# A DRAM copy of the filters in the order of its reading, read back in fewer, taller transfers, the first third at an earlier place

## The chip, the cores and the metric

The kernel runs on one core of a Trainium2 chip. The metric is the device time of one execution in microseconds (us), as the median over several runs. A profile is one profiled execution; its trace has every instruction of every engine and every DMA packet. The engines are named as in the profile: PE (TensorE), PEld (its weight loads), DVE (VectorE), ACT (ScalarE), POOL (GpSimd) and SP (SyncE, which issues DMAs here and computes nothing).

## The reference, cut to what matters

```python
x = (8, 3008, 256); filt_r, filt_i = (1505, 256)      # 3008 = 47 * 64
X = np.fft.rfft(x, axis=1)
y = np.fft.irfft(X * (filt_r + 1j * filt_i), n=3008, axis=1)      # mixing along the sequence
h = y.reshape(24064, 256) @ w_in                       # 256 -> 2048
out = (0.5 * h * (1 + erf(h / sqrt(2)))) @ w_out       # exact GELU, 2048 -> 256
```

Each of 8 batches is transformed along its sequence, multiplied by a filter for each frequency and channel, and transformed back. The result goes through a two-layer network with GELU.

## The kernel before

The transform of length 3008 = 47 x 64 is made of matrix products in stages. A batch of index 1 to 7 goes through these functions:

- `s1` (L375) makes the first products from x, evacuates them through `a_sb` (three buffers, L43) and stores them to a DRAM tile R, 16 transfers a batch (L397). R is read back in another order by `r1` into `b_sb`, four transfers (L403).
- `s2` (L406) makes the spectrum for two of 24 frequency rows at a time, so there are 12 calls a batch, p = 0 to 11. DVE multiplies each by the filters, straight out of PSUM (L414).
- `s3` (L417) and `s3_out` (L434) make the next products and store them through `v_sb` to a second DRAM tile R. `r2` (L442) reads them into `d_sb`, and `s4` (L450) writes y into the ring `y_sb`.

Batch 0 takes another way without DRAM tiles: `c1`, `c1t`, `c2`, `c3`, `c3t`, `c4`. Its twelve products by the filters are in `c2` (L489).

The network follows in 47 tiles of 512 rows: `mm1` (L562) makes `ps_h`, which ACT turns into `g_sb` with GELU, and `mm2` or `mm2_seven` (L575, L642) make the output, which DVE adds up in `ost` and SP stores. The stages of batch b+1 are spread between the products of the network for batch b. That order is written out by hand: each of the 48 x 16 slots of the last loop has a list of calls, which `put(slot, function, arguments)` fills, and each slot ends with a piece of `mm2` and one of `mm1`. Every engine, and SP's queue, runs its instructions in the order in which they are written; nothing is reordered.

The filters lie in one SBUF tile `F` of 128 partitions x 2 (real, imaginary) x 24 rows (`K1`) x 256 channels. Batch 0 and the others need it in different partition orders:

- `load_filters` (L88) loads 64 partitions from the inputs on POOL's queue: rows 0 to 31 direct, 32 to 63 mirrored. `dup_filters` (L110) copies them to partitions 64 to 127. Batch 0 uses F in that order.
- `save_filters` (L97) stores partitions 0 to 63 to a DRAM tile `Fd`, one transfer of 1536 KB on SP (L99).
- `load_filters_again` (L101) reads `Fd` back into F in the order that batches 1 to 7 need: even or odd rows by half of F, each group of 32 rows twice. Each transfer fills 16 partitions from every second row of `Fd`, so a call issues 8 transfers on SP (L107).

The call for rows 0 to 7 stands at slot 13 and that for rows 8 to 23 at slot 17. For batch 1 the four steps of `s1` stand at slots 0, 4, 8 and 12, the first three `r1` at slot 15, and `s2` from slot 22 on. So SP's queue holds, in this order: the save of the filters, 16 stores of R, 8 filter transfers of 128 KB, three loads of `b_sb`, 8 filter transfers of 256 KB, and then an output store, the fourth load of `b_sb`, another output store and the stores of `v_sb`.

F's rows 0 to 7 serve the products p = 0 to 3, rows 8 to 23 the products p = 4 to 11.

Of the kernel before, what the change touches and what calls it, by code (L numbers as in the profile page):

```python
# [12 lines left out]
BF16 = mybir.dt.bfloat16  # L13
# [6 lines left out]
K1 = 24  # L20
# [10 lines left out]
class _Mix:  # L31
# [62 lines left out]
            for q, a in enumerate((direct, mirror)):  # L94
                nc.gpsimd.dma_start(out=self.F[32 * q:32 * q + 32, t, k0:k0 + k, :], in_=a)

    def save_filters(self):  # L97
        self.Fd = self.dram.tile([64, 2, K1, 256], BF16, tag="Fd", name="Fd")
        self.nc.sync.dma_start(out=self.Fd, in_=self.F[0:64])  # L99

    def load_filters_again(self, k0, k):  # L101

        for par in range(2):
            for r in range(2):
                for q in range(2):
                    o = 64 * par + 32 * r + 16 * q
                    self.nc.sync.dma_start(out=self.F[o:o + 16, :, k0:k0 + k, :],  # L107
                                           in_=self.Fd[32 * q + (par ^ q):32 * q + 32:2, :, k0:k0 + k, :])

    def dup_filters(self, eng, k0, k):  # L110
        for k in range(k0, k0 + k, 2):
# [582 lines left out]
def kernel(  # L694
# [9 lines left out]
    m = _Mix(ctx, tc, x, filt_r, filt_i, moe_w_in, moe_w_out, out)  # L704
# [38 lines left out]

    nc.gpsimd.memset(m.vt[:, :, 96, :], 0.0)
    m.dup_filters(nc.gpsimd, 4, 20)
    m.save_filters()


    m.table_2_sin(0)
# [31 lines left out]
    for q in range(1, 7):  # L781
        if q < 6:
            m.c2(2 * q)
            if q + 2 < 6:
                m.c1t(q + 2, (act,))
            if q != 3:
                m.warm_up(2)
            m.c2(2 * q + 1)
        if q < 6:
            m.c3(2 * q - 2)  # L790
            if q == 3:
                m.table_3(2)
                m.table_3_copy(2, True)
            else:
                m.warm_up(1)
        else:
            m.c3(10, 1)
            m.warm_up(1)
            m.c3(11, 1)
# [20 lines left out]
    def put(slot, f, *a):  # L820
        at.setdefault(slot, []).append((f, a))
# [30 lines left out]
    put(7, m.table_4_factors, g)  # L852
    put(11, m.table_u)
    put(11, m.table_4_all, g)
    put(13, m.load_filters_again, 0, 8)
    put(17, m.load_filters_again, 8, 16)
    put(17, m.weight_sums)
    seven = range(1, NT - 1)
# [6 lines left out]
    for s in range((NT + 1) * 16):  # L865
        t, jc = s // 16, s % 16
# [37 lines left out]
```

## Time and profile before

| what | value |
|---|---|
| median of 3 runs | 766.86 us (766.77 to 769.4) |
| the profiled execution's own time | 767.05 us |
| its span, first to last instruction | 765.3 us |
| PE busy | 733.2 us (96%) |
| DVE busy | 585.7 us (77%) |
| ACT busy | 545.5 us (71%) |
| POOL busy | 101.1 us (13%) |
| SP's DMA queue (hardware), share of 16 engines | 36.6% of the span, 73.43 MB |
| POOL's DMA queue (software) | 14.2%, 16.00 MB |
| `Fd<-F`, 1 transfer of 1536 KB | 10.5 us from issue to landing |
| `F<-Fd`, 8 transfers of 128 KB | 5.3 us in the median |
| `F<-Fd`, 8 transfers of 256 KB | 13.7 us in the median |

Times inside a profile are counted from the span's start. A line of a timeline has start, length, engine, source line, operation, what it writes and reads, sizes, the number of instructions merged, and in brackets how long the engine stood idle before it and what ended that. SPq and POOLq mark the issue of a DMA; the time to landing is from issue until the last byte is there. A line of busy times by stage has the stage, its length, then the busy time and count of PE, PEld, DVE, ACT and POOL, the granted share of TensorE's clock, the mean busy share of the 16 DMA engines (over 1 where packets overlap), and GB/s. The chain of waits is followed back from the last instruction, at each step to what released it.

### The profile page before, as it was taken

How to read it: one execution, taken by the hardware profiler on the slowest of the kernel's cores; microseconds unless marked ns; L12 is line 12 of the kernel's file. 1: busy time of each engine (PE TensorE's matmuls, PEld its weight loads, DVE VectorE, ACT ScalarE, POOL GpSimd, SP SyncE). 2: the span in 40 equal slices, each digit the busy share in tenths (PEclk: the TensorE clock that was granted, in tenths of full speed). 3: DMA queues.
4: the chain of work that ended last, by engine and by line, in shares of the span. 5: the costliest groups of instructions: out<-in, count | busy, mean ns of one | idle time of the engine just before them, and what ended most of it. 6: DMA issues, size and time to landing. Idle time of an engine off the chain costs nothing.

```text
span 765.3 us, 20030 instructions
## 1 busy us (share of the span) xinstructions
PE 733.2 (96%) x8252; PEld 520.0 (68%) x8388; DVE 585.7 (77%) x1051; ACT 545.5 (71%) x963; POOL 101.1 (13%) x191
## 2 busy tenths in 40 slices
PE   7986699999999999999999999999999999999998
PEld 4834467667677667676677676766767766777776
DVE  8964597789777996789778797778977799666562
ACT  7873377766787677876778676876678767777773
POOL 7997000012000210002000120001200000000000
PEclk9998899999999999999999999999999999999999
DMA  9999935556625556337544465364662522601011
GB/s 152 220 184 168 182 90 134 142 131 114 159 62 149 120 126 134 88 115 168 114 98 125 138 142 115 90 162 112 114 159 61 148 77 84 140 28 57 29 56 56
DMA packets 91500, 90.71 MB, mean 119 GB/s; under 512 B 7632, under 2 KB 78416, under 8 KB 91088
## 3 DMA queue, kind: packets, MB, share of 16 engines
q1 hardware_dynamic: 83024, 73.43, 36.6%
q0 software_dynamic: 8384, 16.00, 14.2%
q8 instruction: 65, 1.06, 0.6%
q14 instruction: 27, 0.22, 0.1%
HBM read 57.15 MB, written 48.23 MB: 138 GB/s over the span
## 4 chain that ended last, share of the span: by engine, by line
PE 79%; DMA 8%; DVE 4%; issue 3%; POOL 2%; ACT 2%; SPq 1%; DVEq 0%; POOLq 0%; ACTq 0%
PE ps_o L657 35%; PE ps_h L570 33%; PE ps_s L456 3%; PE ps_s L428 3%; PE ps_s L411 2%; DMA F<-Fd 2%; ACT g_sb L573 2%; PE ps_s L387 2%; DVE p L414 2%; DMA x_sb<-in_x_dram 2%; DVE s_sb L627 1%; DMA b_sb<-R 1%; DMA R<-v_sb 1%; DMA d_sb<-R 1%; DMA F<-in_filt_i_dram 1%
## 5 line engine op out<-in xcount | busy, mean ns | idle before, releaser
L573 ACT ACTIVATE g_sb<-ps_h 128x512 f16<-128x512 f32 x752 | 448.2, 598 | 200.8 <-PE ps_h L570 171.0
L570 PE MATMUL ps_h<-y_sb,w_in_sb 128*128 128x512 bf16 (+3 forms) x1468 | 419.7, 366 | 1.2 <-DVE a_sb L297 1.1
L657 PEld LDWEIGHTS <-g_sb 128*128 128x128 f16 x2880 | 190.7, 98 | 85.2 <-issue 16.2
L657 PEld LDWEIGHTS <-s_sb 128*128 128x128 f16 x2160 | 147.9, 98 | 51.5 <-issue 3.1
L657 PE MATMUL ps_o<-w_sums,g_sb 128*128 128x128 f16 x1440 | 125.5, 220 | 6.8 <-DVE g_sb L633 6.0
L570 PEld LDWEIGHTS <-w_in_sb 128*128 128x128 bf16 x1600 | 125.1, 98 | 8.1 <-issue 2.4
L414 DVE TENSOR_TENSOR p<-ps_s,F 128x1024 bf16<-128x1024 f32 x84 | 102.4, 1220 | 33.9 <-PE ps_s L411 16.9
L657 PE MATMUL ps_o<-w_sums,s_sb 128*128 128x128 f16 x1440 | 125.0, 219 | 1.3
L657 PE MATMUL ps_o<-w_out_sb,g_sb 128*128 128x128 f16 x1440 | 118.4, 219 | 1.8
L627 DVE TENSOR_TENSOR s_sb<-g_sb 128x1024 f16<-128x1024 f16 x180 | 118.7, 682 | 0.0
L118 POOL COPY gate<-p 1x1 bf16<-1x1 bf16 x40 | 19.1, 477 | 438.4 <-DVE p L414 438.4
L657 PE MATMUL ps_o<-w_out_sb,s_sb 128*128 128x128 f16 x720 | 62.2, 219 | 0.5
L633 DVE TENSOR_TENSOR g_sb<-s_sb,g_sb 128x1024 f16<-128x1024 f16 x90 | 61.7, 686 | 1.1
L640 DVE TENSOR_TENSOR s_sb<-g_sb 128x1024 f16<-128x1024 f16 x90 | 61.3, 681 | 0.0
L299 DVE TENSOR_SCALAR y_sb<-ps_s 128x376 bf16<-128x376 f32 x56 | 30.5, 545 | 29.0 <-PE ps_s L456 29.0
L297 DVE CAST a_sb<-ps_s 128x512 bf16<-128x512 f32 x60 | 38.5, 685 | 16.8 <-PE ps_s L387 13.9
L456 PEld LDWEIGHTS <-d_sb 96*128 96x128 bf16 x448 | 31.4, 98 | 27.2 <-issue 2.4
L675 DVE TENSOR_TENSOR t_sb<-t_sb,ps_o 128x256 f32<-128x256 f32 x45 | 18.8, 417 | 40.3 <-PE ps_o L657 40.3
L672 DVE TENSOR_TENSOR ost<-t_sb,ps_o 128x256 f32<-128x256 f32 x45 | 18.8, 419 | 31.6 <-PE ps_o L657 31.6
L411 PE MATMUL ps_s<-b_sb,T2p 128*128 128x256 bf16 x168 | 32.6, 276 | 9.0 <-DMA b_sb<-R 8.0
L456 PE MATMUL ps_s<-T4a,d_sb 96*128 96x94 bf16 x448 | 37.4, 206 | 2.6 <-DMA d_sb<-R 1.3
L680 DVE TENSOR_TENSOR ost<-t_sb,ps_o 128x256 f32<-128x256 f32 x90 | 33.6, 414 | 7.4 <-PE ps_o L657 7.4
(149 smaller groups left out, 515.3 us busy)
## 6 DMA issues: line engine op xcount, KB each, us to landing
out_dram<-ost SPq DMA_DIRECT2D x93, 256.0 KB, 2.8
x_sb<-in_x_dram POOLq DMA_DIRECT2D x64, 188.0 KB, 4.0
R<-a_sb SPq DMA_DIRECT2D x112, 96.0 KB, 2.2
b_sb<-R SPq DMA_DIRECT2D x28, 384.0 KB, 4.4
R<-v_sb SPq DMA_DIRECT2D x84, 128.0 KB, 2.4
d_sb<-R SPq DMA_DIRECT2D x56, 192.0 KB, 4.1
F<-Fd SPq DMA_DIRECT2D x8, 256.0 KB, 13.7
Fd<-F SPq DMA_DIRECT2D x1, 1536.0 KB, 10.5
```

Of the source, the lines that this page charges most:

```text
L297: self.nc.vector.tensor_copy(out=out, in_=in_)
L299: self.nc.vector.tensor_scalar(out=out, in0=in_, scalar1=scale, scalar2=None, op0=ALU.mult)
L411: nc.tensor.matmul(ps[:, 256 * i:256 * i + 256], lhsT=self.T2p[:, k].rearrange("p a b c d -> p (a b c d)"), rhs=self.st[b, "b", k // 6][:, ...
L414: nc.vector.tensor_tensor(out=w, in0=ps.unsqueeze(1).to_broadcast([128, 2, 512]), in1=self.F[:, :, 2 * p:2 * p + 2, :].rearrange("p t a b ...
L456: nc.tensor.matmul(ps[:, 94 * i:94 * i + 94], lhsT=d[:, (grp % 2) * 4 + i, 128 * half:128 * half + 128], rhs=self.T4a[:, 4 * grp + i], sta ...
L570: nc.tensor.matmul(ps[:, o:o + n], lhsT=self.w_in_sb[:, dc, jc * 128:jc * 128 + 128], rhs=self.ring[:, dc, off:off + n], start=(dc == 0), ...
L573: nc.scalar.activation(out=self.st["g", t][:, jc, :], in_=ps, func=AF.Gelu)
L627: self.nc.vector.tensor_tensor(out=self.st["s", t][:, i:i + 2], in0=a, in1=b, op=ALU.subtract)
L633: self.nc.vector.tensor_tensor(out=a21[:, k], in0=self.st["s", t][:, k, 0], in1=a22[:, k], op=ALU.add)
L640: self.nc.vector.tensor_tensor(out=self.st["s4", t][:, k], in0=a12[:, k], in1=s2[:, k], op=ALU.subtract)
L657: nc.tensor.matmul(ps[:, (m + 1) % 2, sub, :], lhsT=a[:, i, 128 * sub:128 * sub + 128], rhs=b[:, i], start=i == 0, stop=i == 7)
L680: v(out=c(h, 1 - h), in0=tt, in1=p, op=ALU.add)
```

## The change

`Fd` gets the order in which it is read: first even or odd rows, then direct or mirrored, then 16 rows. `save_filters` takes a range of rows and makes four transfers of 32 partitions each; it is called for rows 12 to 23 and then 0 to 11, so 8 transfers of 192 KB stand for the one. For the mirrored half the rows are stored with even and odd exchanged (`o[:, ::-1]`). `load_filters_again` now fills 64 partitions with one transfer, whose source names its 32 rows twice, by a broadcast dimension in front; a call issues four transfers, of 256 KB each for rows 0 to 7 and of 512 KB for rows 8 to 23. The first call is moved from slot 13 into the loop of batch 0's products, behind the sixth of its twelve, so that in SP's queue its transfers stand between the save and the stores of R. The second call stays at slot 17. The instructions of PE, DVE, ACT and POOL and their order stay as they are.

```diff
-    def save_filters(self):
-        self.Fd = self.dram.tile([64, 2, K1, 256], BF16, tag="Fd", name="Fd")
-        self.nc.sync.dma_start(out=self.Fd, in_=self.F[0:64])
+    def save_filters(self, k0, k):
+
+        if "Fd" not in self.st:
+            self.st["Fd"] = self.dram.tile([2, 2, 16, 2, K1, 256], BF16, tag="Fd", name="Fd")
+        for t in range(2):
+            for q in range(2):
+                o = self.st["Fd"][:, q, :, t, k0:k0 + k, :].rearrange("a i k c -> i a (k c)")
+                if q:
+                    o = o[:, ::-1]
+                self.nc.sync.dma_start(out=o, in_=self.F[32 * q:32 * q + 32, t, k0:k0 + k, :])
 
     def load_filters_again(self, k0, k):
 
         for par in range(2):
-            for r in range(2):
-                for q in range(2):
-                    o = 64 * par + 32 * r + 16 * q
-                    self.nc.sync.dma_start(out=self.F[o:o + 16, :, k0:k0 + k, :],
-                                           in_=self.Fd[32 * q + (par ^ q):32 * q + 32:2, :, k0:k0 + k, :])
+            for t in range(2):
+                i = self.st["Fd"][par, :, :, t, k0:k0 + k, :].rearrange("q i k c -> (q i) (k c)")
+                self.nc.sync.dma_start(out=self.F[64 * par:64 * par + 64, t, k0:k0 + k, :],
+                                       in_=i.unsqueeze(0).to_broadcast([2, 32, k * 256]))
 ...
     m.dup_filters(nc.gpsimd, 4, 20)
-    m.save_filters()
+    for k in (12, 0):
+        m.save_filters(k, 12)
 ...
             m.c3(2 * q - 2)
+            if q == 2:
+                m.load_filters_again(0, 8)
 ...
-    put(13, m.load_filters_again, 0, 8)
     put(17, m.load_filters_again, 8, 16)
```

## The prediction

> **What bounds the kernel now.** I read three things in turn: the share of each engine (TensorE, PE, is busy 733.2 of 765.3 us), then its busy time stage by stage (from 110 to 700 us it is busy for 98 to 99% of every stretch), and then the stage that isn't: 48 to 92 us, where batch 1 waits for data. An instant lost there is lost for good, because each engine's order is fixed and PE has nearly no gap later in which to make it up. So I follow the chain of waits through that stage:
>
> ```profile
> 53.17 4.59 DMA F<-Fd
> 57.83 8.32 DMA b_sb<-R
> 66.16 10.75 DMA F<-Fd
> 76.91 0.60 DVE v_sb L297
> 77.51 0.60 DVE s_sb L627
> 78.11 6.42 issue
> 84.82 1.22 DVE p L414
> ```
>
> The columns are start, length and what held the chain. First third of the filters, then spectra, then the rest of the filters: all on SP's queue, one behind the other. The timeline of SP gives the issues:
>
> ```profile
> 40.47 11.70 SPq L397 DMA_DIRECT2D R<-a_sb  x16
> 52.26 3.67 SPq L107 DMA_DIRECT2D F<-Fd  x8
> 56.02 2.12 SPq L403 DMA_DIRECT2D b_sb<-R  x3
> 58.77 7.69 SPq L107 DMA_DIRECT2D F<-Fd  x8
> ```
>
> The 8 transfers of the first third (128 KB each) stand between the last store of R and the loads of b_sb. PE then stands still for b_sb, VectorE (DVE) for the rest of the filters; these are their lines in the timelines:
>
> ```profile
> 63.39 0.58 PE L411 MATMUL ps_s<-b_sb,T2p 128*128 128x256 bf16 x2 [7.98 <-DMA b_sb<-R]
> 84.82 1.22 DVE L414 TENSOR_TENSOR p<-ps_s,F 128x1024 bf16<-128x1024 f32 x1 [6.71 <-issue]
> 48.44 1.89 DVE L297 CAST a_sb<-ps_s 128x512 bf16<-128x512 f32 x3 [2.80 <-DMA R<-a_sb]
> ```
>
> The third line matters later: DVE already waits 2.80 us for stores of R, since a_sb has three buffers and the fourth step of stage 1 needs the first one back. Last, the rates, from busy times by stage (the last two columns are the DMA engines' share and GB/s):
>
> ```profile
> 24.00:28.00 4.00, 3.92 (x50) 3.10 (x49) 4.00 (x5) 4.00 (x7) 3.94 (x5) 1.00 1.20 352
> 72.00:76.00 4.00, 3.95 (x37) 2.31 (x37) 3.72 (x6) 2.74 (x5) 0.00 (x0) 1.00 1.00 121
> ```
>
> While the filters are written to DRAM (24 to 28 us), 352 GB/s flow, 22 per DMA engine. While they are read back (72 to 76), all 16 engines are busy and move 121 GB/s.
>
> **What the Trainium skill says.** (1) SBUF — State Buffer, "Door 1: The DMA port swizzle": 16 partitions reach 4 of 16 ports and gave 104 GB/s, 64 reach 8 and gave 196. The 121 GB/s above agree; a 64-partition transfer is not in this trace. (2) DMA: Bandwidth & Descriptors, "Why a DMA increments its semaphore by 16 and not by 1": a transfer runs on the largest k up to 16 that divides the slowest dimension (not of size 1) of both of its access patterns; its "Rules for kernel authors" adds that a leading zero-stride broadcast of c copies confines the whole DMA to at most c engines. Every transfer of SP before has k = 16 by that rule, so the trace can't test it. (3) The same page, "Queues, rings and completion order": SP has one ring on each DMA engine, consumed in order. The trace agrees in kind: stores of v_sb issued behind the filters took up to 16.7 us to land, 2.4 in the median.
>
> **The change part by part.**
> The save. One transfer of 1536 KB (issued 21.95, after the last filter load; landed 10.5 us later) becomes eight of 192 KB, 32 partitions to 2 x 16 rows: slowest dimensions 32 and 16, so k = 16. Seven more issues of about 0.45 us (the L397 stores: 302 to 603 ns), on an SP that then has nothing until 40.47. The first need not wait for the last filter load. Cost nothing; the copy lands at about 30 instead of 32.5.
>
> The read back. Sixteen transfers become eight: eight issues less, 8 x 0.36 = 2.9 us of SP. The destination is 64 partitions, but the source is [2, 32, k*256] with step 0 in front. By skill (2), k divides 64 and 2, so k = 2: **two DMA engines carry all of it**, the same two each time. Per engine, the first third is 4 x 256 KB / 2 = 0.52 MB, the rest 4 x 512 KB / 2 = 1.05 MB. Rate of one engine: 22 GB/s from the 352 above, at most 29 (27 GiB/s, the skill's "Specifications" on that page); I take 25, an estimate between. So 21 us (18 to 24) and 42 us (36 to 48) of pure transfer.
>
> The first third, moved. Its wait for the first four products of batch 0 is over by 21.3 (DVE's L500 run: one at 16.03, three more from 17.70 at 1.2 each); the copy is what it waits for: issue at about 30. On the same engines the software queue (x of batch 1, w_out) is busy: over 30 to 48 us its packets took 91.5% of the 16 engines, 16.5 us. Together 30 + 21 + 16.5 = 67.5, less some overlap of the two queues (shares up to 1.42 of an engine stand in the stages): landed at 65, between 56 and 73. Queued behind it on the ring are the stores of R (issued from 40.47): the first four land at 66. SP's transfers also use eight completion semaphores in turn, so the fifth store of R waits for the first filter transfer, the eighth for the fourth: SP stands too. DVE's and ScalarE's fourth evacuation, at 48.4 before, gets its buffer at about 66: +17.6 us.
>
> From there to b_sb. Before, 48.4 to 56.0 for the first issue and 63.4 for PE. Now the last four stores are issued by 69.5 and land at 73; three loads of b_sb follow from 73.5 and land in some 4.4 us (their median): PE starts stage 2 at about 78, +14.6. So 3 us come back, the 3.67 us that the first third no longer takes at 52.26.
>
> The rest of the filters. Issued from about 75, with 2 us of latency, 42 us of transfer and 5 us lent to x of batch 2 (8 x 188 KB; those loads are issued at 67.4 to 71.6 before) and to b_sb: landed at 124. Products 4 to 7 need all four transfers. Before, that product started at 84.82. Work for DVE and PE is there until about 78.1 + 15 = 93; then both stand for some 30 us instead of 6.7. Sum: 124 - 85 = **+39 us**, inside which the +14.6 is already counted. What lies behind on the ring (two stores, the fourth b_sb, v_sb) is needed only after it. After this point nothing changes in the order: no gain, no loss.
>
> The profiled execution took 767.05 us (765.3 and 1.75 around it), 0.19 over the median of 766.86. 767.05 + 39 = 806; I say 805.
>
> Bounds. Low: 29 GB/s and queues that overlap fully: first third landed at 56, b_sb issued at 65.5, the rest landed at 66.5 + 2 + 36 = 104.5: +20, 787. High: 22 GB/s, copy at 32, no overlap: 73, then 84 + 2 + 48 + 8 = 142: +57, 824; at 20 GB/s about 835.
>
> **Rivals.** (a) **All 16 engines carry the read back**: the count is taken from the destination alone, or the source counts as 64 rows. Then it is faster. The first third (1 MB, about 5 us at 196 GB/s) is over by 40; SP issues b_sb 3.7 us earlier and nothing stands ahead of it: PE starts at about 59.5, -4. The rest is 2 MB at 196 GB/s, 11 us, landed by about 70, before DVE asks at 74: the 6.7 us are gone. 767.05 - 10.7 = 756.4; with up to 3 us lost because the first third pushes x and w_out back, 756 to 760. For it: the 16-partition bottleneck is real (121 GB/s). Against it: the skill's rule names exactly this pattern. The deciding point is the rate: not slower from about 2.1 MB / (84.8 - 57) = 75 GB/s, three to four engines; two give 44 to 58.
> (b) **The first third is hidden after all**: queues share so well that it has landed by 48, stores of R aren't held, and only the rest is slow: 57 + 2 + 42 + 5 = 106, +21, 788. Against it: 18 us of transfer at the least beside 16.5 of another queue don't fit in 18.
> (c) **A wash**: 16 engines, but the early transfer delays x and the stores of R by what is gained later, within 4 us of 767. It would need 10 us of collision, where 1 MB costs 5.
>
> **How the numbers follow.** Two engines: 0.84, with (b) in it at 0.08; (a): 0.12; (c): 0.04. Predicted 805. Range 783 to 836: the two-engine case with its bounds, a little beyond at both ends; (a) and (c), 16%, are left out. Faster by over 0.5% (3.8 us, about what a measurement of this kernel can tell from no change) 0.12, within 0.03, slower 0.85 ((c) is split, 0.03 and 0.01).
>
> **What would show it.** Right: filter transfers of the first third that land 10 to 35 us after their issue; the fourth a_sb evacuation near 66; PE's first stage-2 product near 78; product 4 near 124, with about 30 us of DVE and PE idle ahead of it; a low DMA share there, near 2/16, at some 50 GB/s. Wrong: landings of 3 to 10 us at over 100 GB/s in all, and no wait for the filters.

## The result, and the profile after

The changed kernel takes 812.33 us in the median of 4 runs (809.92 to 813.96), against 766.82 us of the kernel before (now 4 runs): the ratio is 1.0585, with a 95% interval of 1.0548 to 1.0622. The profiled execution took 812.77 us, with a span of 811.0. That is 45.7 us more than the profiled execution before.

The chain of waits again, columns start, length, and what held it; "..." marks pieces left out:

```profile
46.08 4.27 SPq L403
50.39 3.12 SPq L403
53.55 1.60 SPq L403
55.19 14.13 DMA R<-a_sb
...
70.19 1.02 PE ps_h L576 x2
...
72.33 1.95 SPq L403
74.33 6.30 DMA R<-a_sb
...
83.88 47.33 DMA F<-Fd
131.42 1.22 DVE p L420
```

Before, three waits for filters and spectra filled 53 to 77 us. Now the stores of R (L403 is now their line) hold the chain from 46 to 69 and again from 72 to 81, and a single wait for filters lasts 47.33 us. The timeline of SP shows why the stores come late:

```profile
19.06 6.56 SPq L106 DMA_DIRECT2D Fd<-F  x8
31.09 12.58 SPq L113 DMA_DIRECT2D F<-Fd  x4
43.71 31.69 SPq L403 DMA_DIRECT2D R<-a_sb  x16
80.89 1.29 SPq L409 DMA_DIRECT2D b_sb<-R  x3
82.23 15.08 SPq L113 DMA_DIRECT2D F<-Fd  x4
```

The sixteen stores of R were issued within 11.70 us before and within 31.69 us now. The four issues of a filter call would take some 2 us at the median of 0.52 us for one; they take 12.58 and 15.08, because the fourth of each call lasted 10.6 and 13.4 us. Two lines of DVE's timeline carry the loss:

```profile
69.44 1.89 DVE L303 CAST a_sb<-ps_s 128x512 bf16<-128x512 f32 x3 [23.38 <-DMA R<-a_sb]
131.42 1.22 DVE L420 TENSOR_TENSOR p<-ps_s,F 128x1024 bf16<-128x1024 f32 x1 [32.21 <-DMA F<-Fd]
```

DVE waited 23.38 us for a buffer of `a_sb` (2.80 before), and 32.21 us for the filters of product 4 (6.71 before). PE stood with it:

```profile
84.26 0.59 PE L417 MATMUL ps_s<-b_sb,T2p 128*128 128x256 bf16 x2 [5.48 <-DMA b_sb<-R]
133.30 0.82 PE L663 MATMUL ps_o<-w_sums,g_sb 128*128 128x128 f16 x6 [31.48 <-DVE g_sb L639]
```

Product 4 starts 131.42 - 84.82 = 46.6 us later than before, and all but 0.9 us of that is still there at the end. The busy times by stage name the resource (last two columns: share of the 16 DMA engines, GB/s):

```profile
56.00:60.00 4.00, 0.00 (x0) 0.00 (x0) 0.00 (x0) 0.00 (x0) 3.77 (x6) 0.50 0.34 93
60.00:64.00 4.00, 0.00 (x0) 0.00 (x0) 0.00 (x0) 0.00 (x0) 3.77 (x5) 0.50 0.17 52
96.00:104.00 8.00, 5.77 (x66) 3.72 (x66) 3.07 (x5) 4.56 (x8) 0.00 (x0) 1.00 0.14 52
```

In the first row stores of R move too. In the other two, where little but filters moves, the DMA engines are busy to a share of 0.14 to 0.17, which is little more than two of sixteen (0.125), and move 52 GB/s. While the rest of the filters was read back before, the share was 1.00 and the rate 121 GB/s.

The trace's records of single DMA packets say the same more directly. The rest of the filters is 256 packets of 8 KB, one for each partition and part. Before, 16 of them were in flight at once for most of the time. Now two are, from 85.6 to 130.7 us, and a third only for 0.9 us in all. The records of completion, which each transfer leaves in the trace, show how the stores of R are held: of the 16 of the first store, fourteen come by 52.0 us and the last two at 67.4 and 68.3, when the first third of the filters is done (67.3).

### The profile page after: what moved, and what is told of

Read it like the earlier page. It is cut to its first block, busy times and chain, and to the rows that moved or that the text cites. A ratio compares the mean times of both kernels' runs of the same rounds, so it can differ in the third digit from the quotient of the medians.

```text
span 811.0 us, 20024 instructions
## 1 busy us (share of the span) xinstructions
PE 735.7 (91%) x8252; PEld 520.7 (64%) x8388; DVE 583.8 (72%) x1051; ACT 545.9 (67%) x963; POOL 99.4 (12%) x191
## 3 DMA queue, kind: packets, MB, share of 16 engines
q8 instruction: 65, 1.06, 0.6%
## 4 chain that ended last, share of the span: by engine, by line
PE 78%; DMA 11%; DVE 5%; SPq 2%; issue 2%; ACT 1%; POOL 0%; DVEq 0%; POOLq 0%; ACTq 0%
PE ps_o L663 33%; PE ps_h L576 32%; DMA F<-Fd 6%; PE ps_s L462 3%; PE ps_s L434 3%; DMA R<-a_sb 3%; PE ps_s L417 2%; PE ps_s L393 2%; DVE p L420 2%; SPq L403 1%; ACT g_sb L579 1%; DVE s_sb L633 1%; DMA d_sb<-R 1%; DMA R<-v_sb 1%; DMA x_sb<-in_x_dram 1%
## 5 line engine op out<-in xcount | busy, mean ns | idle before, releaser
L301 ACT ACTIVATE a_sb<-ps_s 128x512 bf16<-128x512 f32 x52 | 28.4, 598 | 22.0 <-DMA R<-a_sb 21.8
```

What stands on the lines that cost most here:

```text
L301: self.nc.scalar.activation(out=out, in_=in_, func=AF.Copy, scale=1.0 if scale is None else scale)
```

## The experiments

Theory A is that of the prediction: the broadcast dimension in front of the source puts each transfer on two DMA engines, and that is the whole loss. Its rivals: B, the early place of the first third does the harm; C, it isn't the leading dimension that counts but reading each row twice. Later runs ask what the rest of the change is worth.

### Two transfers of 32 partitions instead of one with a broadcast

```diff
-                self.nc.sync.dma_start(out=self.F[64 * par:64 * par + 64, t, k0:k0 + k, :],
-                                       in_=i.unsqueeze(0).to_broadcast([2, 32, k * 256]))
+                for r in range(2):
+                    o = 64 * par + 32 * r
+                    self.nc.sync.dma_start(out=self.F[o:o + 32, t, k0:k0 + k, :], in_=i)
```

> The changed kernel, but each 64-partition transfer with a broadcast source is cut into two of 32 partitions that each read the same 32 rows; places and bytes unchanged. Theory A (a leading dimension of 2 in the source puts a transfer on two DMA engines, and that is the whole loss): all 16 engines carry the read back, its landings fall to 3 to 10 us, stores of R are not held, PE starts stage 2 near 60 us, no wait for filters at product 4; 758 us, 9 under the kernel before. Theory B (the early place does the harm: it pushes x, w_out and the stores of R back): the fourth a_sb evacuation stays late, time over 785 us.

Measured: 753.82 us, ratio to the kernel before 0.9838 (0.9815 to 0.9862), 4 us under the 758 expected. It was run a second time beside a later kernel, with this expectation:

> The kernel with two transfers of 32 partitions, unchanged, on the same chip as the one with its first third at slot 5: 754 us, within 2 of its first measurement.

It took 753.2 us, ratio 0.9805 (0.9782 to 0.9829). In its timeline of SP the same bytes from the same place need 3.78 and 5.04 us of issue:

```profile
31.09 3.78 SPq L115 DMA_DIRECT2D F<-Fd  x8
41.66 12.64 SPq L404 DMA_DIRECT2D R<-a_sb  x16
57.20 1.30 SPq L410 DMA_DIRECT2D b_sb<-R  x3
58.54 5.04 SPq L115 DMA_DIRECT2D F<-Fd  x8
```

The transfers land in 3.8 to 10.9 us, the median is 8.5. The line of product 4 in DVE's timeline has no idle time behind it any more:

```profile
73.59 1.22 DVE L421 TENSOR_TENSOR p<-ps_s,F 128x1024 bf16<-128x1024 f32 x1
```

Theory A holds against B: with the place kept and only the broadcast gone, 812 us become 754, and this kernel is faster than both others. The early transfers may still cost a little: DVE waits 3.9 us for `w_out`, a wait that it does not have in the kernel before.

### Two engines without a broadcast

The DRAM copy gets an unused row behind each 16, so that the 32 source rows are no longer evenly spaced. No row is named twice in a transfer.

```diff
-            self.st["Fd"] = self.dram.tile([2, 2, 16, 2, K1, 256], BF16, tag="Fd", name="Fd")
+            self.st["Fd"] = self.dram.tile([2, 2, 17, 2, K1, 256], BF16, tag="Fd", name="Fd")
...
-                i = self.st["Fd"][par, :, :, t, k0:k0 + k, :].rearrange("q i k c -> (q i) (k c)")
+                i = self.st["Fd"][par, :, 0:16, t, k0:k0 + k, :].rearrange("q i k c -> q i (k c)")
...
```

(The transfers are those of 32 partitions, as in the experiment above.)

> Like the kernel with 32-partition transfers, no broadcast, but the DRAM copy has one unused row between its direct and its mirrored 16 rows, so that the source of a transfer has dimensions 2 x 16 instead of 32. No row is named twice in a transfer. Theory A (the size of the leading dimension counts): two engines again, about 50 GB/s while only filters move, time within 8 us of the changed kernel, 812 us. Theory C (the zero step, or one transfer that reads each row twice, is what is slow): no loss, 758 us.

Measured: 807.2 us, ratio 1.0534 (1.0507 to 1.0561). DVE's waits, in total, times, and longest:

```profile
DVE p L421 <- DMA F<-Fd: 27.0, 1, 27.0
...
DVE a_sb L304 <- DMA R<-a_sb: 22.5, 1, 22.5
```

Both waits of the changed kernel are back, the one for the filters 5 us shorter. The 8 KB packets of the rest of the filters are again two at a time. One unused row in DRAM costs 53 us against the kernel above, so C falls: the size of the leading dimension counts, and no zero step is needed.

### Four engines

An unused row behind each 8 rows makes the source 4 x 8. The save has 16 transfers for it instead of 8.

```diff
...
-                i = self.st["Fd"][par, :, :, t, k0:k0 + k, :].rearrange("q i k c -> (q i) (k c)")
+                i = self.st["Fd"][par, :, :, 0:8, t, k0:k0 + k, :].rearrange("q g i k c -> (q g) i (k c)")
...
```

(The transfers are again those of 32 partitions.)

> Like the kernel with 2 x 16 source rows, but the DRAM copy has an unused row after every 8 rows, so that the source of each 32-partition read back has dimensions 4 x 8; the save is cut into 16 transfers of 16 partitions. Theory A: four DMA engines. Half the time per engine of the changed kernel: the first third landed near 58 us instead of 69, the rest within some 28 us of its issue instead of 49: about 777 us (765 to 785), still over the kernel before. The prediction's own break-even (three to four engines) would have it at 767 or below. If the size of the leading dimension didn't count, 754 us.

Measured: 781.07 us, ratio 1.0187 (1.0166 to 1.0209). The size of the leading dimension orders the kernels: 2 gives 807 to 812 us, 4 gives 781, 32 gives 754. DVE's timeline:

```profile
60.23 1.89 DVE L306 CAST a_sb<-ps_s 128x512 bf16<-128x512 f32 x3 [14.51 <-DMA R<-a_sb]
100.56 1.23 DVE L423 TENSOR_TENSOR p<-ps_s,F 128x1024 bf16<-128x1024 f32 x1 [18.57 <-DMA R<-v_sb]
```

The second line names a store of `v_sb`, but the chain of waits has the filters for most of that time, and the store only for the end of it:

```profile
71.06 26.76 DMA F<-Fd
97.83 2.58 DMA R<-v_sb
```

At most four of the 8 KB packets are in flight, a fifth for 0.4 us in all. The break-even of the prediction, three to four engines, is refuted: four are slower than the kernel before. The save was not untouched here: the destination of its transfers now starts with 8, and each of them left 9 records of completion, where those of the changed kernel left 16. Filter transfers on two engines leave 3 and on four 5, so 9 fits eight engines. The first third is issued at 32.38 us instead of 31.09, so little of the loss can be that.

### The first third back at slot 13, broadcast kept

```diff
-            if q == 2:
-                m.load_filters_again(0, 8)
...
+    put(13, m.load_filters_again, 0, 8)
```

> The changed kernel with its first third back at slot 13, behind the stores of R. Theory A: the two engines need some 63 us for all filters wherever they begin; they begin at about 52 us instead of 31 but the stores of R no longer stand behind them and no time is lost between the two parts, so the last filter lands near 125 us instead of 131: about 806 us. Theory B (the early place does the harm): below 785 us.

Measured: 812.84 us, ratio 1.0614 (1.0584 to 1.0645), so neither number: the loss is as large as in the changed kernel. The timeline of DVE shows that it has only changed its place:

```profile
49.34 1.89 DVE L303 CAST a_sb<-ps_s 128x512 bf16<-128x512 f32 x3 [2.92 <-DMA R<-a_sb]
89.12 1.23 DVE L420 TENSOR_TENSOR p<-ps_s,F 128x1024 bf16<-128x1024 f32 x1 [32.90 <-PE ps_s L417]
...
130.61 1.22 DVE L420 TENSOR_TENSOR p<-ps_s,F 128x1024 bf16<-128x1024 f32 x1 [27.41 <-DMA F<-Fd]
```

The stores of R are free again (2.92 us instead of 23.38), but `b_sb` now lies behind the first third on the two engines, and product 0 comes at 89.12 instead of 84.89. The filters need the time from 53 to 130 us here, where I had expected 125. The packets of the first third alone ran from 54 to 87 us, as long as at the early place (35 to 67); I had put 21 us for them, as if they had the two engines to themselves, but the loads of `b_sb` and of x of batch 2 moved meanwhile. From 88.6 to 129.9 the rest followed.

### Only the place: the kernel before with an early first third

```diff
+            if q == 2:
+                m.load_filters_again(0, 8)
...
-    put(13, m.load_filters_again, 0, 8)
```

> The kernel before with its own save and its own 16-partition transfers, only the first third moved to the changed kernel's place. Theory A: no transfer is on fewer than 16 engines, so no loss: three loads of b_sb are issued some 3.5 us earlier and the rest of the filters lands as much earlier; 762 us (760 to 765). Theory B (the early transfers collide with x, w_out and the stores of R): 767 us or more.

Measured: 764.59 us, ratio 0.9979 (0.9967 to 0.9990): within the 760 to 765 expected, but a gain of only 1.6 us where 762 was written, and below the 3.8 us that I call a difference here. Two lines of DVE's timeline:

```profile
51.79 1.89 DVE L297 CAST a_sb<-ps_s 128x512 bf16<-128x512 f32 x3 [6.10 <-DMA R<-a_sb]
82.08 1.23 DVE L414 TENSOR_TENSOR p<-ps_s,F 128x1024 bf16<-128x1024 f32 x1 [7.39 <-issue]
```

Product 4 starts at 82.08 instead of 84.82; but DVE waits 6.10 us instead of 2.80 for a buffer of `a_sb`, as it would if the early transfers held up the stores of R. What B describes happens in part, and it is small.

### Only the shape: 32 partitions, first third at slot 13

The two-transfer kernel with the place undone.

```diff
-            if q == 2:
-                m.load_filters_again(0, 8)
...
+    put(13, m.load_filters_again, 0, 8)
```

> The kernel with two transfers of 32 partitions for each broadcast one, with its first third back at slot 13. What of its gain is the place, what the shape: if the gain comes mostly from the shape (the wait at product 4 goes), about 758 us; if it comes mostly from the place (b_sb earlier), 763 us or more. PE starts stage 2 near 62 us instead of 60.9.

Measured: 755.2 us, ratio 0.9847 (0.9826 to 0.9868), where the early place had 0.9838 and 0.9805. The gain comes from the shape. For the place there is no more than the 1 to 2 us between the medians, which were taken on different chips and lie within the intervals of the ratios, so a gain from it is not shown.

### A place between the two

```diff
-            if q == 2:
-                m.load_filters_again(0, 8)
...
+    put(5, m.load_filters_again, 0, 8)
```

(applied to the two-transfer kernel)

> The kernel with two transfers of 32 partitions for each broadcast one, with its first third between the two: at slot 5, behind the stores of R of the first two steps of stage 1. w_out is then not pushed back (its wait of 3.9 us on VectorE, 2.2 on TensorE goes) and three loads of b_sb still have nothing but the last stores of R ahead of them: 751 us if both gains add, 754 if the two waits only change places.

Measured: 754.3 us, ratio 0.9819 (0.9797 to 0.9841): no better than the early place on the same chip (0.9805). The two waits only changed places: the one for `w_out` is gone, and PE waits 4.95 us for `b_sb` where it waited 1.54.

### 16 partitions in the new order

The changed kernel's save and early place, with the old shape of the read back.

```diff
-            for t in range(2):
-                i = self.st["Fd"][par, :, :, t, k0:k0 + k, :].rearrange("q i k c -> (q i) (k c)")
-                self.nc.sync.dma_start(out=self.F[64 * par:64 * par + 64, t, k0:k0 + k, :],
-                                       in_=i.unsqueeze(0).to_broadcast([2, 32, k * 256]))
+            for r in range(2):
+                for q in range(2):
+                    o = 64 * par + 32 * r + 16 * q
+                    i = self.st["Fd"][par, q, :, :, k0:k0 + k, :]
+                    self.nc.sync.dma_start(out=self.F[o:o + 16, :, k0:k0 + k, :], in_=i)
```

> The changed kernel's save, order in DRAM and early place, but read back in 16-partition transfers as in the kernel before (8 a call, both parts of the filter in one). Every transfer is on 16 engines. If the width of the destination sets the rate (16 partitions against 32), some 120 GB/s while filters are read back, a wait of about 7 us at product 4 and 764 us, as when only the place was changed. If the order in DRAM (rows read one after the other instead of every second one) sets it, about 754 us.

Measured: 763.11 us, ratio 0.9955 (0.9938 to 0.9972). The rows now follow each other in DRAM, and it doesn't help: with the other order, at the same early place, it was 764.59 us. Busy times by stage while the rest of the filters comes in, first of this kernel:

```profile
66.00:76.00 10.00, 10.00 (x92) 6.63 (x90) 8.04 (x11) 6.61 (x12) 8.88 (x14) 1.00 1.01 137
```

and of the kernel with 32 partitions:

```profile
60.00:70.00 10.00, 9.13 (x67) 6.49 (x68) 7.37 (x9) 5.02 (x9) 9.61 (x12) 1.00 1.04 258
```

Both keep all 16 engines busy; 137 GB/s flow with 16 partitions a transfer, 258 with 32 (other transfers included in both). So the width is what the change had right.

### 64 partitions without a broadcast

The repeated rows are stored twice, in 16 save transfers and 3 MB, so that the source is 64 rows in one step.

```diff
...
-                i = self.st["Fd"][par, :, :, t, k0:k0 + k, :].rearrange("q i k c -> (q i) (k c)")
+                i = self.st["Fd"][par, :, :, :, t, k0:k0 + k, :].rearrange("r q i k c -> (r q i) (k c)")
...
-                                       in_=i.unsqueeze(0).to_broadcast([2, 32, k * 256]))
+                                       in_=i)
```

> The changed kernel's four transfers of 64 partitions a call, but with the repeated rows stored twice in DRAM (16 save transfers, 3 MB instead of 1.5), so that the source is 64 rows in one step and nothing is broadcast. Theory A: 16 engines, no loss: 754 us, within 4 of the kernel with two transfers of 32 partitions, plus up to 3 us for the larger save. If a 64-partition destination were itself what is slow: 800 us or more; if 64 partitions are better than 32: under 751 us.

Measured: 758.07 us, ratio 0.9885 (0.9865 to 0.9904). A 64-partition destination is not slow. The 4 us over the two-transfer kernel fit the longer save: the first third is issued at 38.44 us instead of 31.09, and DVE waits 8.18 us for a buffer of `a_sb` instead of 3.01.

```profile
38.44 7.14 SPq L114 DMA_DIRECT2D F<-Fd  x4
55.83 1.89 DVE L303 CAST a_sb<-ps_s 128x512 bf16<-128x512 f32 x3 [8.18 <-DMA R<-a_sb]
```

The packets of the rest of the filters, the same 256 of 8 KB in every kernel, put the shapes side by side. The rate is worked out from the 2.1 MB and the time from the first packet to the end of the last:

| source rows, partitions filled by a transfer | packets in flight, most often | one packet, median | first to last | rate |
|---|---|---|---|---|
| 2 x 32, 64 (the changed kernel) | 2 | 309 ns | 45.1 us | 47 GB/s |
| 2 x 16, 32 | 2 | 309 ns | 40.2 us | 52 GB/s |
| 4 x 8, 32 | 4 | 309 ns | 29.6 us | 71 GB/s |
| 16, 16 (before) | 16 | 1005 ns | 18.3 us | 115 GB/s |
| 16, 16 (the new order) | 16 | 959 ns | 17.0 us | 123 GB/s |
| 32, 32 | 16 | 621 ns | 10.7 us | 196 GB/s |
| 64, 64 | 16 | 624 ns | 10.3 us | 204 GB/s |

One engine moves 26.5 GB/s where only two or four are at work. With all 16, a packet takes 1.5 to 1.6 times as long with 16 partitions as with 32, and no longer with 64 than with 32.

## Why the prediction was right

- **What bounds the kernel.** Right. Everything that was lost lies in the stretch that the prediction followed, and from product 4 to the end the kernels differ by 0.9 us.
- **Two engines.** Right, and the page's rule decided it: the Trainium skill's DMA: Bandwidth & Descriptors, "Rules for kernel authors", says that an outermost dimension of a size c under 16, a leading broadcast of c copies for one, confines a transfer to at most c engines. The share of 0.14, the 52 GB/s and the two packets in flight agree; so do the kernels with a leading 2 and 4 and no copies.
- **The save.** Right: issued from 19.06 us, nothing waited for it but the first third, which followed at 31.09 where 30 was written.
- **The first third and the stores of R.** Right: the last of its packets ended at 67.0 (65 predicted), and the fourth evacuation came at 69.44 (66 predicted). SP stood for a further reason: I had it wait for semaphores of earlier transfers, but its fourth filter issue alone lasted 10.6 us. The lower bound of this step, 56, is not what its words give: a copy at 30 and 18 us of fully overlapped transfer make 48, which is the case of rival (b).
- **From there to b_sb.** This term was too small: PE's stage 2 at 84.26, 78 predicted. I let the last four stores of R land within 3.5 us and loads of `b_sb` start at 73.5; the chain shows 6.30 us after a last issue at 74.33, and loads from 80.89. At 72 to 80 us the DMA engines were busy to 0.92: x of batch 2, which I had set beside the rest of the filters, was issued from 66.16 and moved beside these stores; that it was what slowed them is likely, but not shown.
- **The rest of the filters.** 47 us after the last issue, 49 from the first, as 2 + 42 + 5 said. It landed 7 us later because it was issued 7 us later (82.23 against 75). That the parts fit so well is in part luck: at 309 ns a packet the transfer would take 40 us, not 42, and the 5 us that I lent to x of batch 2 went elsewhere, since x was through by then. Instead the packets of 84 to 96 us took 430 to 520 ns each in the mean, for which I have no cause. The sum of +39 measured +45.7, inside the stated bounds.
- **Rival (a)** was in the main the right picture of what 16 engines would do, shown by the two-transfer kernel: 753.8 us where 756 to 760 was written. Its loads of `b_sb` were issued no earlier than before (57.20 against 56.02), but with nothing ahead of them PE had its first at 60.87 instead of 63.39, and the wait at product 4 went as written. Its break-even was wrong in two ways. I took it from the rest of the filters alone, but a slow first third also delays the start of the rest: with four engines DVE's fourth evacuation comes at 60.23 instead of 48.44, and the rest is issued at 67.17 where I set 57. And I counted three to four engines for 75 GB/s; four moved the rest at 71. Product 4 came at 100.56 instead of 84.82.
- **Rival (b)** is not what happened: the first third was not hidden. The run at slot 13 adds that freeing the stores of R would not have saved anything either.
- **The Trainium skill's SBUF — State Buffer, "Door 1: The DMA port swizzle"**: 16 partitions against 32 or more behave as the page says: the rest of the filters alone moved at 115 to 123 GB/s with 16 and at 196 with 32. It also says that 64 gain nearly nothing over 32; here they moved at 204, and no gain in time is seen.

## What to carry to other kernels

Before a transfer is made larger, look at the slowest dimension of both of its sides: if one side starts with a small number, be it copies, halves or groups, cut the transfer along that dimension into several. A slow transfer on few engines also delays the later transfers of its queue (here the stores of R landed 9.5 us or more after their issue, before 6.6 or less), and the engine that issues it. What was worth having here is the width of 32 partitions instead of 16, and not one instruction for 64.

## What the runs showed of the hardware that I had not expected

- With two engines, the issue of a filter transfer on SP can itself last long: 10.6 and 13.4 us for the fourth of each call, 18.2 us at slot 13, 7.7 us in the kernel with 2 x 16 rows. With four engines it lasted 0.8 us at most, with 16 it took 0.3 to 1.1. SP does nothing else meanwhile. What holds the issue is not shown.
- After a stall PE is slow for a while. During the 21.67 us without work its granted clock falls to half (0.50 in the stages from 56 to 64 above), and for some 5 us after it pairs of the same products in its timeline take 1.06 us before they take 0.59:

```profile
70.19 1.86 PE L576 MATMUL ps_h<-y_sb,w_in_sb 128*128 128x512 bf16 x4 [21.67 <-DVE a_sb L303]
...
72.70 1.06 PE L576 MATMUL ps_h<-y_sb,w_in_sb 128*128 128x512 bf16 x2
...
75.58 0.59 PE L576 MATMUL ps_h<-y_sb,w_in_sb 128*128 128x512 bf16 x2
```

The mean granted clock over the span of the profiled execution was 0.962 in the changed kernel, 0.991 before and 1.000 with two transfers of 32 partitions. How much of the kernel's time that is worth is not shown: PE was waiting for data in most of this stage, and from product 4 to the end the kernels differ by 0.9 us.
